# W's products in a round of attention: between scores and y and behind the state products, instead of around the turning of x

## The chip, the cores and the metric

One NeuronCore of a Trainium2 chip runs the whole program in one launch. The metric is the device time of that launch in microseconds. The engines are TensorE (PE), VectorE (DVE), ScalarE (ACT), GpSimd (POOL) and SyncE (SP), which issues most DMA transfers.

## The reference

Three layers follow one another on 4 x 768 tokens of width 8 heads x 48:

```python
for t in range(S):                                   # attention with a decaying state per head
    cur = np.einsum('bhd,bhe->bhde', u[None] * kt, vt)
    y[:, :, t] = np.einsum('bhd,bhde->bhe', rt, state + cur)
    state = w[None, :, :, None] * state + np.einsum('bhd,bhe->bhde', kt, vt)
x = y.transpose(0, 2, 1, 3).reshape(B * S, H * D)    # 3072 x 384
# mixture of 8 experts: tokens with x @ w_skip > 0 add gate * (relu(x @ w1[e]) @ w2[e]), e = argmax of x @ w_gate
out = ((x @ w1) * (x @ w2)) @ w3 @ w_out             # second MLP
```

Only the last matrix product can be rearranged ahead of time: `w3 @ w_out` does not depend on the tokens.

## The kernel before

The attention is done in 24 steps of 128 rows: 12 chunks of 64 positions, and for each chunk two groups of two batches (`n = 2 * chunk + group`). A step needs the scores of the chunk (`scores`, tile `sc`, line 371), their copy out of PSUM under a triangular mask (`evac`, tile `Fs`, line 376, on VectorE), the output `y` or `G` as the sum of scores times v (line 425) and of the old state (line 428, `Ss`), and the products that go into the state (`ds_mm`, tile `S`, line 441). `x_out` adds the bonus term and stores the rows (`xg`), `x_trans` turns them (tile `T`, line 457), `logits` multiplies them with the gate (line 470). For some rounds `route_b` (lines 513 to 516) and `place_mm` (line 599) sort tokens to slots.

All these matmuls on heads are 32 passes on half of the array's rows: fp32 runs a matmul in two passes, and each of the 8 heads has one matmul for the upper and one for the lower 64 partitions. Those of W, of the logits and of the turns use all 128 rows.

While attention runs, `w3 @ w_out` is made as well: `W` is 8 rows of 8 matmuls with 384 columns (`w_mm`, line 708, tiles `wp`), 64 matmuls or 128 passes. `keep(4 * k)` issues the next k of these matmuls; where their operands are not ready yet it issues dummies on a zero tile (line 255, 4 for each `keep(4)`). `WK` holds k for the two places of a round: (1, 1) for rounds 0 to 8, (1, 2) for rounds 9 to 21. In rounds 0 to 4 all are dummies. A finished row of W is copied out of PSUM by `w_evac` (line 689, ScalarE).

The order in a round is written out by hand, and every engine runs its instructions in that order: `manual_schedule` takes the program's text as it stands. The loop `for n in range(NT - 2)` at line 772 is such a round: it computes the scores of step n + 1 and the y of step n. What the change touches:

```python
            y_mm(n)                # line 791
            keep(4 * WK[n][0])     # line 792
            run_todo()             # logits of step n - 2, route_b
            if n > 0:
                x_trans(n - 1)     # line 795
            prep_v(n + 1)
            keep(4 * WK[n][1])     # line 797
            w_step(WN[n][1])
            w_evac(0)
            x_out(n)
            ds_mm(n)               # line 801
            place_mm(n % 2)        # line 802
```

Of the kernel before, what the change touches and what calls it, by code (L numbers as in the profile page):

```python
# [43 lines left out]
WK = [(1, 1)] * 9 + [(1, 2)] * 13  # L44
# [15 lines left out]
def fused_kernel(ctx, tc, att, kv, wt, u, wg, we, w3, wo, w12, r, k, v, wu, out):  # L60
# [132 lines left out]
    def load_expert(e, q):  # L193
        raw = stg[(4 * e + q) % 3 // 2].tile([P, 2, 2 * D], F32, name="raw")
        nc.sync.dma_start(out=raw, in_=we[e, :, 2 * q:2 * q + 2, :])
        return raw
# [29 lines left out]
    with tc.manual_schedule():  # L226
# [10 lines left out]
        def load_t(n):  # L237
            nc.sync.dma_start(out=TB[n % 3].rearrange("p a h t -> p (a h t)"), in_=att[n])

        def load_v(n):  # L240
            c, bp = divmod(n, 2)
            nc.sync.dma_start(out=KV[bp][c % 2].rearrange("p a h d -> p (a h d)"), in_=kv[n])
# [47 lines left out]
        for i in range(6):  # L290
            wn = pw[:, i - 1] if i else wc
            n = 1 << i
# [62 lines left out]
        def prep(n):  # L355

            t = TB[n % 3]
            FK = FK_[n] = wk.tile([P, 2, NH, CH], F32, name="FK", bufs=3)
            return nc.vector.tensor_tensor(out=FK, in0=t, in1=UT[:, n // 2 % 2], op=ALU.mult)

        def behind(later, earlier):

            tc.add_manual_dep(later.ins, earlier.ins.name, mybir.DependencyInfo(
                mybir.DependencyClass.Sync, mybir.DependencyReason.DATA), reason="two operands from SBUF each")

        def scores(n):
            FK = FK_[n]
            sc = ps_1.tile([P, 512], F32, tag="sc", name="sc").rearrange("p (h t) -> p h t", h=NH)
            for h in range(NH):
                for m, d in zip(half, dims):  # L370
                    nc.tensor.matmul(sc[m, h], FK[d, 1, h], FK[d, 0, h], start=True, stop=True)  # L371
            return sc

        def evac(n, sc):
            Fs = Fs_[n] = wk.tile([P, NH, CH], F32, name="Fs")
            nc.vector.tensor_tensor(out=Fs, in0=sc, in1=mask[:, None, :].to_broadcast([P, NH, CH]), op=ALU.mult)

        def prep_k(n):

            c, bp = divmod(n, 2)  # L380
            if c < NC - 1:
                kd = kd_[n] = wk.tile([P, NH, HD], F32, name="kd")
                return nc.gpsimd.tensor_tensor(out=kd, in0=KV[bp][c % 2][:, 1], in1=KU[:, c % 2], op=ALU.mult)

        def prep_m(n):

            c, bp = divmod(n, 2)
            m = P_[n] = wk.tile([P, NH, HD], F32, name="m")
            first = nc.gpsimd.tensor_tensor(out=m, in0=KV[bp][c % 2][:, 0], in1=un, op=ALU.mult)
            nc.gpsimd.tensor_tensor(out=m, in0=KV[bp][c % 2][:, 1], in1=m, op=ALU.mult)  # L390
            return first

        def bonus(n):
            z = z_[n] = wk.tile([P, 32], F32, name="z")[:, 0:NH]
            nc.vector.tensor_reduce(out=z, in_=P_.pop(n), axis=AX.X, op=ALU.add)  # L395

        def prep_v(n, eng=None):
            c, bp = divmod(n, 2)
            v, z = KV[bp][c % 2][:, 2], z_.pop(n)
            zv = zv_[n] = wk.tile([P, NH, HD], F32, name="zv")  # L400
            if eng:
                eng.tensor_tensor(out=zv, in0=v, in1=z[:, :, None].to_broadcast([P, NH, HD]), op=ALU.mult)
            else:
                for h in range(NH):
                    nc.scalar.activation(out=zv[:, h], in_=v[:, h], func=AF.Copy, scale=z[:, h:h + 1])  # L405

        def state_copy(n):
            c, bp = divmod(n, 2)
            s = S[bp]
            if c == 0:  # L410
                return
            if c % 2 == 0:
                nc.vector.tensor_tensor(out=s, in0=s, in1=w128[:, :, None].to_broadcast([P, NH, HD]),
                                        op=ALU.mult)
            nc.scalar.copy(out=Ss[bp], in_=s)

        def y_mm(n, tag="y"):

            c, bp = divmod(n, 2)
            v, Fs, FK = KV[bp][c % 2][:, 2], Fs_.pop(n), FK_.pop(n)  # L420
            y = G if n % 2 and n < NT - 2 else ps_1.tile([P, 512], F32, tag=tag, name="y")
            yv = y[:, 0:D].rearrange("p (h d) -> p h d", h=NH)
            for h in range(NH):
                for m in half:
                    nc.tensor.matmul(yv[m, h], Fs[m, h], v[m, h], start=(h == 0), stop=True, skip_group_check=True)  # L425
            for h in range(NH if c else 0):
                for m, d in zip(half, dims):
                    nc.tensor.matmul(yv[m, h], FK[d, 0, h], Ss[bp][d, h], start=False, stop=True,  # L428
                                     skip_group_check=True)
            y_[n] = y  # L430
            if n < NT - 2:
                yb[0] = y
# [19 lines left out]
        def x_trans(n, bank=None):  # L452
            xg = x_.pop(n)
            xb_[n] = T if bank is None else bank
            pT = xb_[n][:, 0:D].rearrange("p (k t) -> p k t", k=ND)
            for k in range(ND):
                nc.tensor.transpose(pT[:, k], xg[:, P * k:P * k + P], ident)
            xT_[n] = wk.tile([P, ND, P], F32, name="xT", bufs=2)
            nc.scalar.copy(out=xT_[n], in_=pT)
# [137 lines left out]
        def place_mm(bp=0):  # L597
            for o, oh, v in pend:
                nc.tensor.matmul(SL[bp][:, o], oh, v, start=False, stop=True, skip_group_check=True)
            pend.clear()  # L600
# [78 lines left out]
        def w_step(k):  # L679
            for _ in range(k):  # L680
                next(wprep, None)
# [3 lines left out]
        def w_evac(k):  # L685

            while k < len(w_out):
                f, ps = w_out[k]
                nc.scalar.copy(out=W[:, f], in_=ps)
                w_out[k:k + 1] = []  # L690

        def w_ready():
            done.update(fresh[0])
            fresh[:] = fresh[1:] + [[]]
# [21 lines left out]
        def idle_mm():  # L716
            if spare[0] is None and w_out:
                w_evac(0)
            dummy(DQ)
            dummy(DQ)  # L720

        def keep(k):

            due[0] += k
            while due[0] > 0:
                if next(wmm, None):
                    due[0] -= 4
                else:
                    idle_mm()
                    due[0] -= 2  # L730
# [28 lines left out]
        def run_todo(late=False):  # L759
            now, todo[:] = sorted(todo, key=lambda x: x[0] is not logits), []  # L760
            for fn, args in now:
                if late and fn is route_b:
                    todo.append((fn, args))
                    continue
                fn(*args)
                if fn is logits_out:
                    if args[0] in last_of:
                        todo.append((route_a, (last_of[args[0]],)))
                elif fn in NEXT:
                    todo.append((NEXT[fn], args))  # L770

        for n in range(NT - 2):
            w_ready()
            if n == NT - 3:
                raws = {q: load_expert(0, q) for q in range(2)}
            if n + 4 < NT:
                load_t(n + 4)
            fk = prep(n + 2)
            state_copy(n + 1)
            sc = scores(n + 1)  # L780
            behind(prep_k(n + 1) or prep_m(n + 2), fk)
            if n < NT - 3:
                prep_m(n + 2)
            evac(n + 1, sc)
            bonus(n + 1)
            if n == NT - 3:
                bonus(NT - 1)
            next(more_consts, None)
            w_step(WN[n][0])
            w_ready()  # L790
            y_mm(n)
            keep(4 * WK[n][0])
            run_todo()
            if n > 0:
                x_trans(n - 1)
            prep_v(n + 1)
            keep(4 * WK[n][1])
            w_step(WN[n][1])
            w_evac(0)
            x_out(n)  # L800
            ds_mm(n)
            place_mm(n % 2)
            if n + 4 < NT:
                load_v(n + 4)
            if n < NT - 3:
                place(3)
            w_step(WN[n][2])
            run_todo(n < NT - 3)
            if n > 0:
                todo.append((logits, (n - 1,)))  # L810
# [662 lines left out]
```

## Time and profile before

| | before |
|---|---|
| median of 3 runs | 633.9 us (633.12 to 634.04) |
| profiled execution, its own time | 637.01 us |
| profiled execution, span | 635.3 us |
| mean granted clock of PE | 0.991 |
| PE busy | 614.5 us, 97% of the span |
| DVE busy | 464.1 us, 73% |
| ACT busy | 290.7 us, 46% |
| attention, from the first scores to the scores of the last step | 7.6 to 161.8 us |

The profiled execution is a single one, 3.1 us above the median of the runs; busy times and spans come from it. The rounds of attention lie between 10 and 162 us; the tail of attention follows to some 183 us, then the experts to 335 us and the second MLP to the end. In the rows further down, a block of equal instructions is one line: start, length, engine, source line, operation, written tile, read tiles, form, count, and in brackets the idle time before it with what ended it. Blocks overlap a little, since matmuls are pipelined; so the distance from one start to the next is the block's cost, not its length.

### The profile page before, as it was taken

How to read it: one execution, taken by the hardware profiler on the slowest of the kernel's cores; microseconds unless marked ns; L12 is line 12 of the kernel's file. 1: busy time of each engine (PE TensorE's matmuls, PEld its weight loads, DVE VectorE, ACT ScalarE, POOL GpSimd, SP SyncE). 2: the span in 40 equal slices, each digit the busy share in tenths (PEclk: the TensorE clock that was granted, in tenths of full speed). 3: DMA queues.
4: the chain of work that ended last, by engine and by line, in shares of the span. 5: the costliest groups of instructions: out<-in, count | busy, mean ns of one | idle time of the engine just before them, and what ended most of it. 6: DMA issues, size and time to landing. Idle time of an engine off the chain costs nothing.

```text
span 635.3 us, 15258 instructions
## 1 busy us (share of the span) xinstructions
PE 614.5 (97%) x6313; PEld 545.4 (86%) x6313; DVE 464.1 (73%) x820; ACT 290.7 (46%) x705; POOL 141.3 (22%) x140
## 2 busy tenths in 40 slices
PE   7999998999999999999998999999999999999996
PEld 6888877888769999989997989988988988988985
DVE  7699998986477799999956954863863863863760
ACT  2555644534355667666534542443443442442430
POOL 3856465463040232232132300000000000000000
PEclk9799998999999999999999999999999999999999
DMA  8889988575148768877321002002002002000001
GB/s 310 358 280 378 326 291 286 177 252 198 45 127 301 277 230 296 287 241 272 112 75 57 1 17 84 1 18 83 2 18 84 1 17 84 2 18 33 1 2 55
DMA packets 26941, 90.40 MB, mean 142 GB/s; under 512 B 4009, under 2 KB 10729, under 8 KB 25840
## 3 DMA queue, kind: packets, MB, share of 16 engines
q1 hardware_dynamic: 24816, 84.11, 38.1%
q0 software_dynamic: 2048, 5.24, 2.5%
q8 instruction: 51, 0.84, 0.5%
q14 instruction: 26, 0.21, 0.1%
HBM read 77.61 MB, written 12.39 MB: 142 GB/s over the span
## 4 chain that ended last, share of the span: by engine, by line
PE 78%; DVE 11%; DMA 5%; issue 3%; ACT 1%; SPq 0%; POOL 0%; DVEq 0%; ACTq 0%
PE po L1237 16%; PE xy L1196 11%; PE za L1196 10%; PE zb L1196 8%; PE wp L708 6%; PE hp L923 6%; PE y L942 5%; DMA TB<-in_att 3%; DVE elo L87 3%; PE sc L371 3%; PE S L441 2%; PE y L425 2%; PE y L428 1%; PE G L428 1%; DVE hl L927 1%
## 5 line engine op out<-in xcount | busy, mean ns | idle before, releaser
L1178 DVE TENSOR_TENSOR C<-st,za 128x512 f32<-128x512 f32 x47 | 32.3, 687 | 69.7 <-ACT st L1213 69.6
L87 DVE TENSOR_TENSOR elo<-raw,ehi 128x768 fp32r<-128x768 f32 x64 | 60.4, 948 | 4.1 <-ACT ehi L86 4.0
L1237 PE MATMUL po<-pl,W_hi 128*128 128x512 f32 (+1 forms) x152 | 58.1, 383 | 0.0
L1237 PE MATMUL po<-ph,W_hi 128*128 128x512 f32 (+1 forms) x152 | 58.0, 382 | 0.0
L1237 PE MATMUL po<-ph,W_lo 128*128 128x512 f32 (+1 forms) x152 | 57.6, 379 | 0.0
L923 PE MATMUL hp<-xh,ehi 128*128 128x240 f32 x192 | 54.5, 286 | 3.0 <-DVE hl L927 2.4
L1213 ACT COPY st<-xy 128x256 f32<-128x256 f32 x47 | 17.6, 374 | 81.8 <-PE xy L1196 81.8
L86 ACT CAST ehi<-raw 128x768 fp32r<-128x768 f32 x64 | 52.7, 829 | 2.1 <-DMA raw<-in_we 2.1
L1196 PE MATMUL xy<-bxh,w12h 128*128 128x256 f32 x188 | 53.3, 283 | 0.0
L1196 PE MATMUL xy<-bxl,w12h 128*128 128x256 f32 x188 | 53.1, 282 | 0.0
L1196 PE MATMUL xy<-bxh,w12l 128*128 128x256 f32 x188 | 53.1, 282 | 0.0
L923 PE MATMUL hp<-xl,ehi 128*128 128x240 f32 x192 | 52.6, 276 | 0.0
L923 PE MATMUL hp<-xh,elo 128*128 128x240 f32 x192 | 52.4, 274 | 0.0
L708 PE MATMUL wp<-wo_s,w 128*128 128x384 f32 x128 | 51.7, 515 | 0.1
L405 ACT ACTIVATE zv<-KV,z 128x48 f32<-128x48 f32 x184 | 44.0, 327 | 8.0 <-DVE z L395 6.9
L1196 PE MATMUL za<-bxh,w12l 128*128 128x512 f32 x141 | 45.1, 320 | 0.0
L1196 PE MATMUL za<-bxh,w12h 128*128 128x512 f32 x141 | 45.0, 319 | 0.0
L1196 PE MATMUL za<-bxl,w12h 128*128 128x512 f32 x141 | 44.7, 317 | 0.0
L942 PE MATMUL y<-ehi,hh 128*128 128x384 f32 (+1 forms) x128 | 43.3, 339 | 0.0
L942 PE MATMUL y<-elo,hh 128*128 128x384 f32 (+1 forms) x128 | 43.2, 338 | 0.0
L942 PE MATMUL y<-ehi,hl 128*128 128x384 f32 (+1 forms) x128 | 43.1, 337 | 0.0
L923 PEld LDWEIGHTS hp<-xh,ehi 128*128 128x128 f32 x192 | 36.1, 189 | 7.9 <-DVE hl L927 6.9
(249 smaller groups left out, 1671.5 us busy)
## 6 DMA issues: line engine op xcount, KB each, us to landing
raw<-in_we SPq DMA_DIRECT2D x32, 768.0 KB, 5.1
KV<-in_kv SPq DMA_DIRECT2D x24, 576.0 KB, 5.3
TB<-in_att SPq DMA_DIRECT2D x24, 512.0 KB, 7.3
raww<-in_w SPq DMA_DIRECT2D x8, 1024.0 KB, 7.5
raw<-in_w SPq DMA_DIRECT2D x8, 768.0 KB, 6.6
xm<-xg SPq DMA_DIRECT2D x48, 96.0 KB, 3.3
out<-ob SPq DMA_DIRECT2D x17, 256.0 KB, 2.0
x<-xm SPq DMA_DIRECT2D x20, 192.0 KB, 2.8
```

Source lines behind the costliest of these rows:

```text
L86: nc.scalar.copy(out=hi, in_=raw)
L87: (eng or nc.vector).tensor_tensor(out=lo, in0=raw, in1=hi.bitcast(F32), op=ALU.subtract)
L371: nc.tensor.matmul(sc[m, h], FK[d, 1, h], FK[d, 0, h], start=True, stop=True)
L405: nc.scalar.activation(out=zv[:, h], in_=v[:, h], func=AF.Copy, scale=z[:, h:h + 1])
L425: nc.tensor.matmul(yv[m, h], Fs[m, h], v[m, h], start=(h == 0), stop=True, skip_group_check=True)
L708: nc.tensor.matmul(ps, w3[:, g], wo_s[:, g], start=(g == 0), stop=(g == NF - 1))
L923: nc.tensor.matmul(hp, a, b, start=(i == 0), stop=(i == 8))
L942: nc.tensor.matmul(ys[e, t], a[:, P * t:P * t + ROWS[t]], b[:, D:2 * D], start=(f == 0 and i == 0), stop=(f == NF - 1 and i == 2))
L1178: nc.vector.tensor_tensor(out=halves(C[:, 0]), in0=st[:, 0:2], in1=halves(za), op=ALU.add)
L1196: nc.tensor.matmul(o, a, m, start=first and i == 0, stop=(i == 2), skip_group_check=True)
L1213: nc.scalar.copy(out=st[:, 0], in_=X)
L1237: nc.tensor.matmul(po, a[:, f, c], b[:, t], start=(i == 0), stop=(i == 3 * NF - 1))
```

## The change

The first `keep` of a round goes ahead of `y_mm`, behind the scores. The second goes from ahead of `ds_mm` to behind `place_mm`, so that what it issues stands ahead of the next round's scores. Nothing is added or left out, and the numbers of `WK` are the same.

```diff
             w_step(WN[n][0])
             w_ready()
+            keep(4 * WK[n][0])
             y_mm(n)
-            keep(4 * WK[n][0])
             run_todo()
             if n > 0:
                 x_trans(n - 1)
             prep_v(n + 1)
-            keep(4 * WK[n][1])
             w_step(WN[n][1])
             w_evac(0)
             x_out(n)
             ds_mm(n)
             place_mm(n % 2)
+            keep(4 * WK[n][1])
```

On PE, a plain round late in attention (here one that writes `G`; `wp` are W's products, `sc` the scores, `T` the turn, `S` the state; each line gives the count of matmuls, of which every fp32 one runs in two passes):

```order
 L371 MATMUL sc<-FK 64x64 x16
+L708 MATMUL wp_121<-wo_s,w_1092 128x384
 L425 MATMUL G<-KV_0_113,Fs 64x48 x16
 L428 MATMUL G<-Ss_116,FK 64x48 x16
-L708 MATMUL wp_121<-wo_s,w_1092 128x384
 L470 MATMUL G<-wgs,xT 128x9 x3
 L457 MATMUL T<-ident,xg 128x128 x3
+L441 MATMUL S_195<-KV_0_113,kd 48x48 x16
 L708 MATMUL wp_121<-wo_s,w_1092 128x384 x2
-L441 MATMUL S_195<-KV_0_113,kd 48x48 x16
 L371 MATMUL sc<-FK 64x64 x16
```

W's first matmul moved from behind y to ahead of it, and the state products moved up from behind W's other two matmuls to directly behind the turn.

On PE, the end of a round in which tokens are placed (line 599, the last of its three placing matmuls, ahead of the next round's scores):

```order
 L599 LDWEIGHTS s_oh
 L599 MATMUL S_194<-s_v,s_oh 128x80
+L708 MATMUL wp_121<-wo_s,w_1092 128x384 x2
 L371 MATMUL sc<-FK 64x64 x16
+L708 MATMUL wp_121<-wo_s,w_1092 128x384
 L425 MATMUL G<-KV_0_113,Fs 64x48 x16
```

W's two matmuls now stand between the placing and the scores, and the third behind the scores.

On ACT, one of three places where the copy of a finished row of W (line 689) goes down by a round (`L` are logits, `Ss` the state's copy, `xT` the turned x, `zv` the bonus term):

```order
+L473 COPY L<-G 128x9
+L415 COPY Ss_116<-S_195 128x384
+L459 COPY xT<-T 128x384
+L405 ACTIVATE zv<-KV_0_113,z 128x48 x8
 L689 COPY W<-wp_121 128x384
-L473 COPY L<-G 128x9
-L415 COPY Ss_116<-S_195 128x384
-L459 COPY xT<-T 128x384
-L405 ACTIVATE zv<-KV_0_113,z 128x48 x8
```

The copy passed one round's copies of logits, state and turned x and its bonus term. On DVE only the numbers of buffers differ, and POOL and SP have the same order as before.

## Rows read from the trace of the kernel before

**Rows 1.** Stretches: length, busy PE, PEld, DVE, ACT, POOL, clock, DMA share, GB/s.
```profile
41.00:55.00 14.00, 13.95 (x336) 12.10 (x338) 13.89 (x17) 9.58 (x31) 8.32 (x8) 1.00 0.93 339
...
75.00:95.00 20.00, 19.94 (x403) 16.12 (x399) 19.72 (x35) 9.60 (x30) 10.13 (x9) 1.00 0.84 289
...
125.00:145.00 20.00, 20.00 (x438) 17.02 (x438) 16.53 (x30) 8.04 (x33) 10.61 (x10) 1.00 0.72 239
```

**Rows 2.** Timeline of PE in round 16, scores to the next round's scores.
```profile
119.17 1.11 PE L371 MATMUL sc<-FK 48*64 48x64 f32 x32
120.11 1.09 PE L425 MATMUL y<-KV,Fs 64*64 64x48 f32 x32
121.03 1.10 PE L428 MATMUL y<-Ss,FK 48*64 48x48 f32 x32
122.06 0.91 PE L708 MATMUL wp<-wo_s,w 128*128 128x384 f32 x2
122.81 0.73 PE L470 MATMUL y<-wgs,xT 128*128 128x9 f32 x6
123.40 0.53 PE L457 MATMUL T<-ident,xg 128*128 128x128 f32 x3
123.76 1.46 PE L708 MATMUL wp<-wo_s,w 128*128 128x384 f32 x4
125.14 0.92 PE L441 MATMUL S<-KV,kd 64*48 64x48 f32 x32
125.90 1.11 PE L371 MATMUL sc<-FK 48*64 48x64 f32 x32
```

**Rows 3.** Timeline of PE in round 5, where W has two passes between T and S.
```profile
45.87 0.81 PE L708 MATMUL wp<-wo_s,w 128*128 128x384 f32 x2
46.61 0.92 PE L441 MATMUL S<-KV,kd 64*48 64x48 f32 x32
```

**Rows 4.** Timeline of PE in attention's tail: y behind W, logits behind y.
```profile
167.01 1.14 PE L425 MATMUL y<-KV,Fs 64*64 64x48 f32 x32
167.98 1.10 PE L428 MATMUL y<-Ss,FK 48*64 48x48 f32 x32
169.00 0.84 PE L470 MATMUL G<-wgs,xT 128*128 128x9 f32 x6
```

**Rows 5.** Timeline of PE at the end of round 11, with placing.
```profile
86.74 0.92 PE L441 MATMUL S<-KV,kd 64*48 64x48 f32 x32
87.60 0.28 PE L599 MATMUL S<-s_v,s_oh 128*128 128x80 bf16 x3
87.81 1.15 PE L371 MATMUL sc<-FK 48*64 48x64 f32 x32
```

**Rows 6.** Timeline of PE in round 3, dummies around logits and turn.
```profile
32.12 0.61 PE L255 MATMUL wp<-zb 128*128 128x256 bf16 x4
32.57 0.73 PE L470 MATMUL G<-wgs,xT 128*128 128x9 f32 x6
...
33.52 0.60 PE L255 MATMUL wp<-zb 128*128 128x256 bf16 x4
34.05 0.92 PE L441 MATMUL S<-KV,kd 64*48 64x48 f32 x32
```

**Rows 7.** Timeline of PE from 40 to 106 us: its waits, and what follows the longest.
```profile
40.98 1.15 PE L371 MATMUL sc<-FK 48*64 48x64 f32 x32 [0.43 <-DVE Fs L376]
...
55.90 1.13 PE L428 MATMUL G<-Ss,FK 48*64 48x48 f32 x31 [0.37 <-issue]
...
62.34 0.56 PE L425 MATMUL y<-KV,Fs 64*64 64x48 f32 x13 [0.50 <-issue]
...
99.79 0.37 PE L428 MATMUL G<-Ss,FK 48*64 48x48 f32 x5 [1.80 <-issue]
...
101.79 2.59 PE L708 MATMUL wp<-wo_s,w 128*128 128x384 f32 x4
104.31 1.37 PE L441 MATMUL S<-KV,kd 64*48 64x48 f32 x32
```

## Prediction

> **What bounds the kernel now.** I read the busy time by stretches first, then TensorE's timeline inside single rounds, then the waits at its idle spots. The reader should see in [rows 1] that in three stretches between 41 and 145 us TensorE (PE) is hardly ever free: 13.95 of 14.00, 19.94 of 20.00 and 20.00 of 20.00 us, at the full granted clock. VectorE (DVE) is just as full early (13.89 of 14.00, 19.72 of 20.00) and has room later (16.53 of 20.00). So a round of attention lasts as long as PE's own instructions, and what the change costs or saves must be read from how PE's blocks follow one another. [rows 2] are round 16: seven blocks between the scores at 119.17 and the next at 125.90, 6.73 us, with no wait. I call a block small if its matmuls use half of the array's rows (scores `sc`, the two halves of `y`, state products `S`) and full if they use all 128 (W's products `wp`, logits at line 470, turns `T` at line 457, the dummies at line 255). Today a round has one pair of switches: small to full from `y` to `wp`, full to small from `wp` to `S`. The order shown above has three pairs in a plain round: sc|wp|y, y|logits and T|S, S|wp|sc.
>
> **What a pair of switches costs.** The same instructions are timed by the distance from one block's start to the next's.
> Small to full: the 32 passes of the first half of y take 121.03 - 120.11 = 0.92, the 32 of the second 122.06 - 121.03 = 1.03 [rows 2], 0.11 more where a full block follows. Two passes of W entered from y take 122.81 - 122.06 = 0.75. Their own pace: four passes between T and S take 125.14 - 123.76 = 1.38 [rows 2], two in the same place 46.61 - 45.87 = 0.74 [rows 3], so a pass is 0.32 and two are 0.64 to 0.65. Entering costs 0.10 more. Together 0.21.
> Full to small: 0.74 - 0.65 = 0.09 on the full side [rows 3], and on the small side the first half of y takes 167.98 - 167.01 = 0.97 where W stands before it, against 0.92: 0.05 [rows 4]. Together 0.14.
> A pair with fp32 weights is thus **0.35 us**. Two of the new neighbours already occur in the tail: W before y (above), and the logits straight after y, again 169.00 - 167.98 = 1.02 against 0.92 [rows 4].
> Bounds for one pair: below, a round in which the placing matmuls (line 599, bf16) stand between S and sc: 87.81 - 86.74 = 1.07 [rows 5] against 125.90 - 125.14 = 0.76 without them [rows 2], 0.31 more for one pair and three short matmuls; even if those take 0.1 together a pair is 0.2. Above, 0.40: 0.35 plus a rounding step of 0.01 in each of the differences. I take 0.35, since it is read from the very blocks that are moved.
>
> The Trainium skill (TensorEngine Tiling, section Tiling Modes, Key Properties) says that changing the tiling mode drains TensorE; it gives no time. Another of its pages (TensorE: Matmul & The Clock Gate, Part 2, the drain step) puts a drain at about 128 cycles; at 2.4 GHz that is 0.053 us for a switch, an estimate, and the 29 pairs below would come to 3.1 us instead of 10.2. The trace agrees that a switch costs, and not on that size: 0.35 for a pair.
>
> **The change, part by part.** The first `keep` moves from behind y to ahead of it; the second from ahead of S to behind S and the placing. No instruction is added or removed.
> 1. Rounds 5 to 21 run real W products. In twelve of these seventeen rounds the number of pairs goes from one to three. In the other five (11, 12, 17, 18, 21) the placing matmuls already make S|place|sc a pair ([rows 5] is one), and W now stands directly behind them, so there it goes from two to three. 12 x 2 + 5 x 1 = 29 pairs x 0.35 = **+10.2**. All of it is on the path, since PE has no idle time there [rows 1].
> 2. Rounds 1 to 4 run four dummies at each `keep`. A pair around dummies: 0.11 on leaving y as above; the four take 0.45 entered from y and 0.53 left into S [rows 6], so at least 0.08 on leaving; 0.05 on the small side as above. I take 0.25 (ends 0.24 and 0.35). Before there is one such pair; after there are two, and one y|logits, T|S pair at 0.35: 0.60 a round, 2.4 for four. Round 0 waits for loads and hides its share. PE reaches the scores at 40.98 with 0.43 us to wait for DVE's Fs [rows 7], which absorbs that much: **+2.0**.
> 3. Two short stalls of PE in the middle of y, 0.37 before 55.90 and 0.50 before 62.34, end on "issue", no engine's work [rows 7]. Both fall in the run S, sc, y, y, in which 128 small matmul passes and as many weight loads are issued in 0.76 + 0.94 + 0.92 + 1.03 = 3.65 us [rows 2] with nothing long between them. The change cuts this run with W on either side of sc, so I take both away: **-0.87**. Bounds: 0 and -0.87.
> 4. The long stall, 1.80 before 99.79, also "issue", and behind it the half clock: four passes at 101.79 take 104.31 - 101.79 = 2.52 instead of 1.38 [rows 7]. Nothing I can read says whether a shifted program meets it, so it stays in the sum, and its removal (1.80 + 1.14, and 0.45 in the S block behind, busy 1.37 [rows 7] instead of 0.92 [rows 2]: 3.4) makes one end of the range.
> 5. ScalarE copies a finished piece of W one round later. It is off the path: ACT is busy 8.04 of 20.00 us [rows 1] and W has two banks. Without that cover a copy would cost PE under 1 us each time; three are moved. The orders of SP and POOL do not move, so no transfer is issued past another. No semaphore wait is added: sc still comes after Fs and FK, with more time for DVE before it.
>
> Sum: 10.2 + 2.0 - 0.9 = **+11.3**. The profiled execution took 637.0 (span 635.3) and would become 648.3; it stands 3.1 above the median of the runs, 633.9, to which I add the same: **645.2 us**.
>
> **The rivals.**
> A, the long stall and its half clock are gone: 645.2 - 3.4 = 641.8. For it: it is the same sort of stall as the two short ones, and the run before it is cut. Against: it is five times as long, and may be absent from unprofiled runs anyway. 0.17.
> B, VectorE paces the early rounds, so that PE's switches there are free. DVE is 99% busy from 41 to 55 and from 75 to 95 us [rows 1]. Rounds 5 to 12 would lose 14 pairs, 4.9, and rounds 1 to 4 their 2.0: 638.3. Against: PE is as full, and waited 0.43 in all for Fs in this stretch [rows 7]. 0.06.
> C, the other side, **faster**: in the run of small blocks the supply of instructions is what PE lacks, and the next block's loads are fetched early enough to hide a switch. Then the change costs nothing, and the three stalls with the half clock, 0.87 + 3.4 = 4.3, are won: 629.6. It decides where a pair costs under 4.3 / 37 = 0.12, 37 being the 29 pairs and the 8 early ones. For it: the turns pass to W at full pace, T to wp 0.36 for three turns [rows 2], so loads are hidden between full blocks. Against: 0.35 measured at exactly the other kind of border, and never under 0.2. 0.05.
> The Trainium skill's rule behind C (TensorE: Matmul & The Clock Gate, Part 2, the LDWEIGHTS step) is that the engine pulls weight loads ahead of running matmuls where row groups do not conflict or the background buffer is the target. The trace agrees between full blocks, and not where a small block precedes: there the first two passes of W took 0.10 longer.
> D, gains and costs cancel: a pair costs about 0.12 and the stalls go, 633 to 635. The diff does act in every round, so "no effect" needs such a balance. 0.03.
> E, the clock: the added gaps let PE fall to half clock in a stretch of the rounds, as behind 99.79. One such fall costs 1.6 (1.14 + 0.45), two 3.2: 648.4, and more if it comes often. For it: 6 gaps a round instead of 2. Against: the fall of [rows 7] came after 1.80 us without work, while a gap at a switch is 0.1 to 0.2. 0.09.
>
> **How the numbers follow.** The forecast, with its terms at other values (0.32 to 0.38 a pair, the short stalls kept), is 644 to 647 and has 0.60. Rivals A to E hold 0.40. The range takes in the forecast, A, and E with two falls: **640.5 to 648.5**; B, C, D and the far part of E, about 0.17, are outside. A measurement of this kernel can tell about 0.2% (1.3 us) from no change. Faster by more than that is C: 0.05. Within: D, 0.03. Slower: 0.92.
>
> **What would show it.** Right: a plain round late in attention takes 7.4 instead of 6.73 us; sc to wp reads 1.05 instead of sc to y 0.94; T to S about 0.45, S to wp about 0.87; the logits behind y take 0.70 instead of 0.59; no waits of PE on DVE after 41 us; everything behind attention is shifted whole. Step 3 is wrong if "issue" stalls remain inside y. Wrong altogether: rounds of 6.7 us (C), rounds under 7 before 95 us with waits on Fs (B), or half clock in [rows 1]'s stretches (E).

## The result and the profile after

The changed kernel takes **642.2 us** (median of 5 runs, 641.06 to 643.91) beside 633.2 of the kernel before (633.12 to 634.04, 5 runs on the same chip): ratio 1.0139, 95% interval 1.0122 to 1.0156, so 9.0 us slower. The forecast was 645.2 with a range of 640.5 to 648.5. The profiled execution of the changed kernel took 642.80 us, its span is 641.1; that of before 637.01 and 635.3. The two profiles differ by only 5.8, because the one of before holds the long stall and the half clock of [rows 7], which a second profile of it doesn't have (experiments 8 and 11 are second profiles of both kernels).

First the stretches that answer to [rows 1], of the kernel after (length, busy PE, PEld, DVE, ACT, POOL, granted clock, DMA share, GB/s):

```profile
41.00:55.00 14.00, 14.00 (x317) 11.44 (x316) 13.89 (x18) 8.20 (x26) 8.32 (x8) 1.00 0.90 301
75.00:95.00 20.00, 20.00 (x393) 15.13 (x390) 19.73 (x37) 10.63 (x36) 10.06 (x10) 1.00 0.79 280
125.00:145.00 20.00, 20.00 (x393) 15.52 (x389) 15.89 (x26) 9.06 (x36) 11.30 (x11) 1.00 0.61 199
```

PE is now busy without a gap in all three, and does less: 393 matmuls from 125 to 145 us where there were 438. A slower kernel with a busier engine: the share of busy time says nothing about the pace here, because a switch is counted as busy. Weight loading (PEld) went the other way, 17.02 to 15.52.

PE's timeline in round 16 of the kernel after (start, duration, engine, line, operation, output<-input, count), which answers to [rows 2]:

```profile
121.78 1.15 PE L371 MATMUL sc<-FK 48*64 48x64 f32 x32
122.86 0.91 PE L708 MATMUL wp<-wo_s,w 128*128 128x384 f32 x2
123.70 1.13 PE L425 MATMUL y<-KV,Fs 64*64 64x48 f32 x32
124.67 1.10 PE L428 MATMUL y<-Ss,FK 48*64 48x48 f32 x32
125.70 0.84 PE L470 MATMUL y<-wgs,xT 128*128 128x9 f32 x6
126.39 0.53 PE L457 MATMUL T<-ident,xg 128*128 128x128 f32 x3
126.84 0.92 PE L441 MATMUL S<-KV,kd 64*48 64x48 f32 x32
127.69 1.56 PE L708 MATMUL wp<-wo_s,w 128*128 128x384 f32 x4
129.18 1.15 PE L371 MATMUL sc<-FK 48*64 48x64 f32 x32
```

From start to start, with [rows 2] in brackets: scores 1.08 (0.94), W's two passes 0.84 (0.75), y 0.97 and 1.03 (0.92 and 1.03), logits 0.69 (0.59), turns 0.45 (0.36), state products 0.85 (0.76), W's four passes 1.49 (1.38). The round takes 7.40 instead of 6.73. Seven of the eight blocks have a new neighbour on one side or on both and became 0.05 to 0.14 longer; the second half of y, which has a full block behind it as before, kept its 1.03.

The end of round 11, a round with placing, on the same timeline; it answers to [rows 5]:

```profile
89.46 0.92 PE L441 MATMUL S<-KV,kd 64*48 64x48 f32 x32
90.32 0.28 PE L599 MATMUL S<-s_v,s_oh 128*128 128x80 bf16 x3
90.43 1.53 PE L708 MATMUL wp<-wo_s,w 128*128 128x384 f32 x4
91.90 1.15 PE L371 MATMUL sc<-FK 48*64 48x64 f32 x32
```

Placing passes to W after 0.11 where it passed to the scores after 0.21. Such a round takes 7.49 or 7.50 instead of 7.04 to 7.09 (one of the five in before, round 12, took 7.30).

Of the waits of [rows 7] none is left. PE waits on Fs only at the scores of rounds 0 and 1. The summed waits of PE from 0 to 185 us (line, releaser: us in total, times, longest):

```profile
PE sc L371 <- DVE Fs L376: 1.3, 2, 1.1
```

No "issue" row is in that view, and no wait lies in rounds 5 to 21. The scores of round 5, at 40.98 in [rows 7], stand here without a wait:

```profile
42.37 1.15 PE L371 MATMUL sc<-FK 48*64 48x64 f32 x32
```

### The profile page after: what moved, and what is told of

Its sections match the earlier page's. It is cut to its first block, busy times and chain, and to the rows that moved or that the text cites. A ratio compares the mean times of both kernels' runs of the same rounds, so it can differ in the third digit from the quotient of the medians.

```text
span 641.1 us, 15258 instructions
## 1 busy us (share of the span) xinstructions
PE 623.6 (97%) x6313; PEld 545.2 (85%) x6313; DVE 461.1 (72%) x820; ACT 290.5 (45%) x705; POOL 141.6 (22%) x140
## 4 chain that ended last, share of the span: by engine, by line
PE 81%; DVE 11%; issue 2%; DMA 2%; ACT 1%; POOL 0%; SPq 0%; DVEq 0%; ACTq 0%; POOLq 0%
PE po L1237 15%; PE xy L1196 11%; PE za L1196 10%; PE zb L1196 8%; PE wp L708 6%; PE hp L923 5%; PE y L942 5%; PE sc L371 4%; DVE elo L87 4%; PE S L441 3%; PE y L425 2%; PE G L425 2%; PE y L428 2%; DVE hl L927 2%; PE G L470 2%
## 5 line engine op out<-in xcount | busy, mean ns | idle before, releaser
L961 POOL DMA_INDIRECT xm<-yo,sidx x16 | 23.3, 1454 | 88.3 <-DVE yo L958 74.0
```

The source lines that it names most:

```text
L961: ins = nc.gpsimd.indirect_dma_start(out=xm[:, :], out_offset=bass.IndirectOffsetOnAxis(ap=sidx[0:n, j, 1:2], axis=0), in_=yo, in_offset=N ...
```

## The experiments

In every diff the lines are those of the loop over the rounds, against the kernel before. Where a kernel has several runs, several of the kernel before stand beside them, on the same chip. "Own pace" of a round means that no block in it stalls.

### 1. The first product of W alone is moved

```diff
+            keep(4 * WK[n][0])
             y_mm(n)
-            keep(4 * WK[n][0])
```

> Only the first group of W's products moves (to between scores and y); the second stays ahead of the state products. Theory (a pair of switches between half-array and full-array matmuls costs 0.34 us): every one of rounds 5 to 21 gets exactly one pair more, 17 x 0.34 = 5.8, rounds 1 to 4 about 0.25 each less the 0.4 that PE waited, small stalls inside y partly gone (0.9 to 2): +4 to +6, 637 to 639. A plain round late in attention 7.07 instead of 6.73. Rival (the cost is the delay of the scores by W's products in front of them, which DVE's mask copy and so the next round pays): here nothing stands in front of the scores, so 0 to +1.

Measured: 637.59 us beside 633.91, ratio 1.0051 [1.0017, 1.0084], +3.7. PE's timeline late in attention:

```profile
117.27 1.11 PE L371 MATMUL sc<-FK 48*64 48x64 f32 x32
118.31 0.91 PE L708 MATMUL wp<-wo_s,w 128*128 128x384 f32 x2
119.16 1.14 PE L425 MATMUL y<-KV,Fs 64*64 64x48 f32 x32
120.13 1.10 PE L428 MATMUL y<-Ss,FK 48*64 48x48 f32 x32
```

Scores to W 1.04 instead of 0.94, W 0.85 instead of 0.75, the first half of y 0.97 instead of 0.92, the logits behind it 0.69 instead of 0.59: +0.35 for one more pair. The total is just under the forecast of +4 to +6. The round takes 7.08, one with placing 7.40, both 0.35 above before. So a half of the change has half of its cost in each round.

### 2. The second product of W alone is moved

```diff
-            keep(4 * WK[n][1])
...
             place_mm(n % 2)
+            keep(4 * WK[n][1])
```

> Only the second group moves (to behind the state products and the placing). Theory: one pair more in the 12 plain rounds, none in the 5 with placing: 12 x 0.33 = 4.0, rounds 1 to 4 about 0.3 each less the wait of 0.4: +4 to +5, 637 to 638.5; rounds with placing keep 7.05 to 7.1. Rival (delay of the scores): all of the change's +9 is here.

Measured: 635.99 us, ratio 1.0012 [0.9990, 1.0034], +2.1 by the medians, with the interval reaching to no change; the verdict rests on the timeline:

```profile
121.05 0.53 PE L457 MATMUL T<-ident,xg 128*128 128x128 f32 x3
121.50 0.92 PE L441 MATMUL S<-KV,kd 64*48 64x48 f32 x32
122.35 1.56 PE L708 MATMUL wp<-wo_s,w 128*128 128x384 f32 x4
123.84 1.15 PE L371 MATMUL sc<-FK 48*64 48x64 f32 x32
```

A plain round takes 7.06 (+0.33: the turns 0.45 instead of 0.36, S 0.85 instead of 0.76, W 1.49 instead of 1.38, and the scores behind it 0.98 instead of 0.94). A round with placing takes 7.15, +0.11, where I had put 0: placing already made that pair, but W behind it is not quite as cheap as W behind the turns. If W in front of the scores had delayed the next round as such, this kernel alone would have carried the 9 us. It doesn't: in a plain round the two halves add up, 0.35 + 0.33 = 0.68 beside 0.67. The whole times don't add up: the medians give 3.7 + 2.1 = 5.8 of the 9.0, and this half stays below its forecast of +4 to +5. A good part of the gap lies in rounds 5 to 10, where each half alone has room that both share: they take 40.10 us in experiment 1 and 40.23 here beside 39.72 in before (experiment 8), 0.4 and 0.5 more, though six pairs cost 2.0 to 2.1.

### 3. Both products move, but stay together

```diff
-            keep(4 * WK[n][0])
...
+            keep(4 * WK[n][0])
             keep(4 * WK[n][1])
```

> Both groups stand together between the turning of x and the state products: W moved as far as in the change, but the number of switches is that of the kernel before. Theory: within 1 us of before, a plain round 6.73. Rival (what counts is that W's products are spread over the round, for the clock or for the instruction supply): slower by some us, with half clock or stalls that end on issue.

Measured: 633.66 us, 0.25 below before by the medians; the ratio, 0.9968 [0.9948, 0.9989], is lower than the medians say; 14 of before's 35 runs there lie above 635, and none of this kernel's 12. W stands in one block between the turns and S:

```profile
119.06 2.10 PE L708 MATMUL wp<-wo_s,w 128*128 128x384 f32 x6
121.09 0.92 PE L441 MATMUL S<-KV,kd 64*48 64x48 f32 x32
```

Here W's first product is moved past logits and turns, and ScalarE's copy of a piece shifts as it does in the change, but the number of pairs in a round stays one. The round stays at 6.73. Moving W costs nothing; a new border does.

### 4. Placing ahead of the state products

```diff
+            place_mm(n % 2)
             ds_mm(n)
-            place_mm(n % 2)
```

> The kernel before with the placing matmuls ahead of the state products, so that they follow W directly. Theory: one pair less in the 5 rounds with placing, which take about 6.75 to 6.8 instead of 7.04 to 7.1: -1.5 us, 631.7. Rival (the placing costs what its own three matmuls take, or waits for DVE's lanes in its new place): no change or slower.

Measured: 632.88 us, ratio 0.9968 [0.9944, 0.9992], 1.0 below before by the medians. A round with placing:

```profile
134.02 1.46 PE L708 MATMUL wp<-wo_s,w 128*128 128x384 f32 x4
135.31 0.27 PE L599 MATMUL S<-s_v,s_oh 128*128 128x80 bf16 x3
135.51 0.92 PE L441 MATMUL S<-KV,kd 64*48 64x48 f32 x32
136.27 1.11 PE L371 MATMUL sc<-FK 48*64 48x64 f32 x32
```

The forecast was -1.5 and 6.75 to 6.8 a round, a little too much. S now passes to the scores after 0.76 as in a plain round, and the placing costs 0.20 behind W less the 0.09 that W's exit no longer has. The round takes 6.84 instead of 7.05; five of them make 1.05. This takes a pair out where the change puts pairs in, and it is the kernel that beats both with the rounds to show for it (experiment 3's interval lies below 1 too, but its rounds are as long as before, so an interval this close to 1 proves little by itself).

### 5 to 7. One added matmul, at three kinds of place

A matmul of zeros with an output that nobody reads: a full one among small ones, a small one in the same place, and a full one among full ones.

```diff
+            nc.tensor.matmul(T[:, 448:512], zb[:, 0:P], zb[:, 0:64], start=True, stop=True)
             y_mm(n)
```

> The kernel before with one more matmul in every round, on a zero tile with all 128 rows and 64 columns in bf16, between scores and y; its result is not used. Theory (a pair of switches costs, whatever the full matmul does): 0.2 to 0.3 in each plain round, 6.95 to 7.0 instead of 6.73, and +3 to +4 in all, because rounds 1 to 9 hide part behind DVE. Rival (what costs is W's long matmul standing in front of y, or fp32 weights that are loaded late): one short bf16 matmul costs 0.03 a round, under +1.

```diff
+            nc.tensor.matmul(T[0:64, 448:512], zb[0:64, 0:64], zb[0:64, 0:64], start=True, stop=True)
             y_mm(n)
```

> The same place and the same 64 columns, but with 64 rows and 64 weight columns, half of the array as its neighbours. Theory: no switch, so 0.03 to 0.06 a round and under +1 in all. Rival (any foreign matmul between scores and y costs, for a wait or for the bank it writes): as much as with all 128 rows.

```diff
             keep(4 * WK[n][0])
+            nc.tensor.matmul(T[:, 448:512], zb[:, 0:P], zb[:, 0:64], start=True, stop=True)
```

> The full matmul of 128 rows and 64 columns beside W's first product behind y, among full blocks. Theory: no switch is added, 0.03 to 0.06 a round, under +1 in all. Rival (the matmul itself or its bank costs): as much as between scores and y.

Measured, beside 633.67: 641.07 us for the full one among small ones (ratio 1.0098 [1.0071, 1.0124]), 638.0 for the small one (1.0052 [1.0029, 1.0074]), 635.24 for the full one among full ones (1.0025 [1.0000, 1.0050]). All three medians are above their forecasts (+3 to +4, under +1, under +1) and the first two well above what the rounds give. The three profiled executions each hold a stretch at half clock (last section); of the other runs only the mean granted clock is known, and in most runs of the first two it is as low as in the profiled ones, 0.987 to 0.992. The lowest runs are 638.09, 634.55 and 634.03. So the price is read from the rounds, from PE's timeline. Full among small:

```profile
121.12 1.11 PE L371 MATMUL sc<-FK 48*64 48x64 f32 x32
122.16 0.20 PE L791 MATMUL T<-zb 128*128 128x64 bf16 x1
122.29 1.14 PE L425 MATMUL y<-KV,Fs 64*64 64x48 f32 x32
123.26 1.10 PE L428 MATMUL y<-Ss,FK 48*64 48x48 f32 x32
```

Small among small:

```profile
120.02 1.11 PE L371 MATMUL sc<-FK 48*64 48x64 f32 x32
120.96 0.19 PE L791 MATMUL T<-zb 64*64 64x64 bf16 x1
120.97 1.13 PE L425 MATMUL y<-KV,Fs 64*64 64x48 f32 x32
121.89 1.14 PE L428 MATMUL y<-Ss,FK 48*64 48x48 f32 x32
```

Full among full:

```profile
120.80 0.91 PE L708 MATMUL wp<-wo_s,w 128*128 128x384 f32 x2
121.55 0.19 PE L793 MATMUL T<-zb 128*128 128x64 bf16 x1
121.58 0.81 PE L470 MATMUL y<-wgs,xT 128*128 128x9 f32 x6
122.25 0.52 PE L457 MATMUL T<-ident,xg 128*128 128x128 f32 x3
```

The scores to the full matmul take 1.04 instead of 0.94, it takes 0.13, and the first half of y 0.97 instead of 0.92: +0.28. With the small matmul the same three read 0.94, 0.01 and 0.92, and the whole round is longer by 0.05 (6.78). With the full one between W and the logits: 0.75, 0.03 and 0.67 for the logits instead of 0.59, +0.11. The same matmul is thus 2.5 times as dear between small blocks as between full ones, and a small one there is nearly free. So most of the price comes with the change of kind, not with one more instruction. Not all of it does: of the 0.11, which has no change of kind in it, 0.08 is the logits' own time. Behind this short full matmul they take 0.67, nearly the 0.69 that they take straight behind y in the changed kernel, and behind W's long matmuls 0.59. So what is booked to a switch at the logits may be a first weight load that a short matmul ahead does not cover; that was not tested. Nor was it tested whether rows or columns make the kind: the full matmul has 128 of both, the small one 64.

### 8 and 11. Both kernels profiled again

> The kernel before once more, for a second profile of it. If the long stall before 99.79 us with its half clock belongs to that one execution, it is absent here and the attention ends some 3 us earlier; rounds 5 to 9 then show short stalls that end on issue, or waits for DVE. If it belongs to the program, it is there again at the same place.

> The changed kernel once more, for a second profile. If the half clock of rounds 1 to 3 (16.3 to 23.1 us in its first profile) is that execution's, it is absent here: the scores of round 5 start near 41 us after a wait for Fs instead of at 42.37 without one, and the span is about 1.3 shorter, 639.5 to 640.

Measured: 632.95 us with a span of 631.1 (clock 0.998) for the kernel before, 641.24 with 639.4 (clock 0.999) for the changed one. Neither has a half-clock stretch or the long stall, and they differ by 8.3, close to the 9.0 of the medians. So this pair is the one to take apart. The kernel before, PE's timeline in rounds 5 to 10:

```profile
40.80 1.15 PE L371 MATMUL sc<-FK 48*64 48x64 f32 x32 [0.97 <-DVE Fs L376]
...
54.98 1.44 PE L428 MATMUL G<-Ss,FK 48*64 48x48 f32 x32
56.36 0.91 PE L708 MATMUL wp<-wo_s,w 128*128 128x384 f32 x2
...
66.75 0.38 PE L425 MATMUL G<-KV,Fs 64*64 64x48 f32 x6
67.40 0.95 PE L425 MATMUL G<-KV,Fs 64*64 64x48 f32 x25 [0.26 <-issue]
...
68.20 1.14 PE L428 MATMUL G<-Ss,FK 48*64 48x48 f32 x31
...
79.27 0.92 PE L441 MATMUL S<-KV,kd 64*48 64x48 f32 x32
80.52 1.15 PE L371 MATMUL sc<-FK 48*64 48x64 f32 x32 [0.33 <-DVE Fs L376]
```

The changed kernel, summed waits of PE on Fs from 40 to 185 us:

```profile
PE sc L371 <- DVE Fs L376: 1.2, 1, 1.2
```

That one wait is at the scores of round 5, which come at 40.83, beside 40.80 before: rounds 0 to 4 cost nothing here, since both kernels end them waiting for Fs. Rounds 5 to 10 take 39.72 before (40.80 to 80.52) and 42.02 after (40.83 to 82.85), +2.30; rounds 11 to 21 take 76.11 and 82.21, +6.10.

In the late stretch six plain and five placing rounds at +0.67 and +0.43 make 6.2, and 6.10 is there. In rounds 5 to 10 six at +0.67 make 4.0, and only 2.30 is there. The rest is what before lost against its own pace: the second half of y takes 56.36 - 54.98 = 1.38 instead of 1.03 in round 7, the first half 1.07 instead of 0.92 in round 8 and 68.20 - 66.75 = 1.45 in round 9, together 1.03 in the middle of y, and S to the scores takes 80.52 - 79.27 = 1.25 instead of 0.76 in round 10 with a wait on Fs, and 0.06 more in round 5: together 0.55. The changed kernel has neither; its rounds 5 to 10 run at their own pace, 6.76 four times, 7.58 and 7.40.

Whatever makes y stall, the kernel before could hardly have been faster here, because of VectorE. Its copy of Fs that the scores of round 11 wait for, first in the kernel before, then in the changed one:

```profile
79.78 0.68 DVE L376 TENSOR_TENSOR Fs<-sc,mask 128x512 f32<-128x512 f32 x1
79.80 0.68 DVE L376 TENSOR_TENSOR Fs<-sc,mask 128x512 f32<-128x512 f32 x1
```

From 40 to 98 us every instruction of VectorE starts at the same time in both kernels, within 0.04 us, though PE falls behind by 3.2 us in that time (scores of round 13 at 94.68 and 97.84): VectorE keeps its own pace there and waits for PE in neither. In the kernel before, the scores of round 11 start 0.06 behind the end of that copy, 79.78 + 0.68 = 80.46. Had y not stalled, PE would have waited there instead. In the changed kernel they come 2.4 behind it. So 1.7 of the 4.0 that the new pairs cost in rounds 5 to 10 is hidden behind VectorE.

### 9 and 10. The change in the first or the last rounds alone

Experiment 9 makes both moves where n < 9, experiment 10 where n >= 9:

```diff
+            if n < 9:
+                keep(4 * WK[n][0])
             y_mm(n)
-            keep(4 * WK[n][0])
+            if not (n < 9):
+                keep(4 * WK[n][0])
...
-            keep(4 * WK[n][1])
+            if not (n < 9):
+                keep(4 * WK[n][1])
...
             place_mm(n % 2)
+            if n < 9:
+                keep(4 * WK[n][1])
```

> The change in rounds 0 to 8 alone, the old order from round 9. Theory (switches cost 0.67 a round, but VectorE is nearly as full as PE up to round 10 and its mask copies hold PE up anyway): the 0.67 is seen in rounds 5 to 8 as 6.76 instead of 6.1, yet waits for Fs and short stalls go in exchange, so +0.5 to +1.5 in all. Rival (every pair of switches is on the path, in early rounds too): 8 pairs in rounds 5 to 8 at 0.34 and 1 to 2 for the rounds of dummies: +4 to +5.

> The change in rounds 9 to 21 alone. Theory: 8 plain rounds x 0.67 and 5 with placing x 0.43 = 7.5, less the 0.3 to 0.5 that PE waits for Fs around round 10: +6.5 to +7.5, so nearly all of the change's +8 to +9. Rival (all pairs count alike): +7.5 here and the rest of some 4 in the early half.

Measured, beside 633.76: 634.39 for the early rounds (ratio 1.0004 [0.9986, 1.0022], +0.6), 643.99 for the late ones (1.0152 [1.0103, 1.0202], its two lowest runs 640.46 and 640.72). In the profile of experiment 9 rounds 5 to 8 take 6.76 each, 27.03 beside 25.01 in experiment 8, and rounds 9 and 10, in the order of before, take 6.95 and 6.73 where experiment 8 has 7.48 and 7.23. So of the +2.0 by which rounds 5 to 8 are longer, 1.0 comes back in the two rounds behind them, where PE, 1.8 us later than in experiment 8, has neither a stall in y nor a wait on Fs, in the old order. In experiment 10 rounds 9 to 21 take 97.15 (69.91 to 167.06) beside 90.82: +6.33, about what eight plain and five placing rounds cost, 7.5, less the 1.07 that experiment 8 loses in rounds 9 and 10.

The 644 of experiment 10 is more than the whole change costs. Its stretches show why (columns as above):

```profile
30.00:41.00 11.00, 8.75 (x200) 7.82 (x199) 10.96 (x13) 4.45 (x15) 6.70 (x12) 1.00 0.72 240
41.00:52.00 11.00, 11.00 (x155) 9.22 (x155) 10.93 (x13) 6.88 (x24) 5.86 (x5) 0.54 0.89 318
```

Its PE timeline at the scores of round 5 and of round 6:

```profile
40.82 1.20 PE L371 MATMUL sc<-FK 48*64 48x64 f32 x32 [1.50 <-DVE Fs L376]
...
51.32 1.43 PE L371 MATMUL sc<-FK 48*64 48x64 f32 x32
```

Round 5, which is in the order of before in this kernel, took 10.50 instead of 6.19 because the granted clock fell to the lower level, 1.2 instead of 2.4 GHz, behind a wait of 1.50 for Fs. These 4.3 and the 6.33 make 10.6 of the 11.0 by which its span, 642.1, exceeds that of experiment 8. The cost of the late rounds is thus 6.3, not 10; the two lowest runs, 6.7 and 7.0 above before, lie in the forecast of +6.5 to +7.5, the median does not.

## Why the prediction was right, and where its steps were off

**The pair of switches (0.35): right in mechanism and near in size.** Three ways to make pairs gave 0.35 (experiment 1), 0.33 (2) and, for both, 0.67 a plain round; moving W without a new border gave 0 (3); removing the pair at the placing gave -0.21 (4), just at the lower bound that had been read from [rows 5]. A round with placing was taken as one more pair net, 0.35, and costs 0.43, because W behind the placing costs 0.11. The Trainium skill (TensorEngine Tiling, section Tiling Modes, Key Properties) says that a change of tiling mode drains TensorE. The runs agree that a change of kind costs, 0.28 for a full matmul among small blocks against 0.11 among full ones. The estimate from the other page of the Trainium skill (TensorE: Matmul & The Clock Gate, Part 2, the drain step), 3.1 us for 29 pairs, is a third of the 10.2 that the rounds show. What a switch is made of, a drain or the next weight load that starts late, was not separated; with bf16 weights the added full matmul costs 0.28, with W's fp32 a pair costs 0.33 to 0.35, so the kind of load may have a part in it.

**Item 1 (+10.2): right in the price, wrong in "all of it is on the path".** Twelve rounds at 0.67 and five at 0.43 are 10.2. In rounds 11 to 21 all of it is on the path (+6.10 of 6.2); in rounds 5 to 10 VectorE hides 1.7 of 4.0. PE's full share of busy time in [rows 1], 13.95 of 14.00, was read as no idle time; but a block that is stretched counts as busy.

**Item 2 (+2.0 in rounds 1 to 4): the size was wrong.** In the first pair of profiles it is +1.39 (scores of round 5 at 42.37 against 40.98), and two of the rounds there do grow from 5.58 to 6.16, the 0.60 of the prediction. But in that pair both kernels had run most of round 1 at half clock, 16 to 23 us, which had put PE behind and used up its slack. In experiments 8 and 11 the same scores come at 40.80 and 40.83 and wait 0.97 and 1.22 for Fs: VectorE sets that time, and the term is 0. The 0.43 us of wait in [rows 7] that I subtracted was the slack of an execution that had been slowed.

**Item 3 (-0.87, the short stalls): the stalls went, but the mechanism was not shown and the gain is not theirs.** The stalls inside y are gone in every round with W on both sides of the scores (changed kernel, experiment 9). They are gone as well in the old order where PE runs later against VectorE: in rounds 9 and 10 of experiment 9, and nearly in experiment 4, where a half clock brought PE to the scores of round 5 at 43.19 and rounds 5 to 10, with no placing in them, lost only 0.5 against their own pace. So that W's place in the run of small blocks removes them was not shown. Nor does their going win time, since VectorE sets the scores of round 11. How large they are must be read from the lengthening of the block, not from the idle time marked "issue": [rows 7] marks 0.37 and 0.50, experiment 8 marks only 0.26, while its blocks of y grew by 1.03. That the supply of instructions is what those rows stand for was argued from the trace; no run altered it alone. Where the prediction took 0.87 off for stalls, the runs show 1.7 hidden behind VectorE.

**Item 4, rival A (the long stall): it belonged to one execution.** Experiment 8 is the same program as before without it. So the profiled execution of before carried some 4 us that experiment 8 does not have (spans 635.3 and 631.1), 3.6 of them in the round of the long stall, 10.41 instead of 6.77, for which the prediction had 3.4; the prediction was right to leave it in both its sides, taking 3.1 off at the end to reach the median. Rival A's 641.8 is nearer to the result than the forecast, but not for its reason: it takes off once more what the median of before had not held.

**The sum.** 10.2 + 0 - 1.7 = +8.5, beside +8.3 in the second pair of profiles and +9.0 by the medians. The prediction's +11.3 is 2.8 above that sum, 2.0 of it from item 2 and 0.8 because VectorE hid 1.7 where 0.87 had been put for the stalls, and 2.3 above the medians. Both errors come from VectorE's pace up to round 10, and both made the forecast too high.

**The other rivals.** B (VectorE paces the early rounds), given 0.06, holds for rounds 1 to 4 and, in part, for 5 to 10, where 1.7 of 4.0 is hidden: 3.7 of the 6.9 that it took off, so that the result lies between the forecast and B's 638.3. What stood against it, that PE is as full and waits only 0.43 for Fs, overlooked the stretched blocks. B doesn't hold for all pairs, since from round 5 on the changed kernel's rounds are at their own pace, with DVE as busy as before, 39.45 of the 40.00 us from 41 to 81 us in both. C (the switches are hidden, faster) and D (cancelled) fall: no new pair of W's in a plain round cost under 0.33, and of the 4.3 that C counted on, the long stall was not in the median, and the short ones had lain in time that VectorE set. E (half clock in attention) is real as a risk of any of these kernels, experiments 4, 5, 6, 7 and 10 had it, but the changed kernel's two profiles have none of it in rounds 5 to 21.

## What to carry to other kernels

When PE is full, write its program as a string of blocks by the part of the array that they use and count the borders: here each pair of borders costs a third of a microsecond, and where full blocks are put together (W beside logits and turns, placing beside W) it is paid once a round. Read that price from distances between block starts, since a slower switch looks like a busier engine. An engine that is busy all the time can still have slack: here the start times of VectorE, the same in both kernels up to 98 us, showed that PE had it. And take slack, stalls and clock from more than one execution before they enter a sum.

## What the runs showed of the hardware that was not expected

A stretch at the lower clock comes in some executions and at different places: between 16 and 24 us in the first profiles of both kernels (mean granted clock 0.76 from 14 to 28 us in either) and in experiments 6 and 7, behind 99.79 in [rows 7], 28.6 to 38.5 in experiment 4, 40.6 to 44.1 in experiment 7, 41.8 to 52.0 in experiment 10, 42.5 to 52.7 in experiment 5, 71.2 to 78.0 in experiment 6. Before the two falls near 42 PE had waited 1.31 (experiment 5) and 1.50 us (experiment 10) for Fs at the scores of round 5; with waits of 0.97, 1.22 and 1.23 at the same scores (experiments 8, 11 and 9), but also of 1.32, 1.39 and 1.44 (experiments 1, 2 and 6), the clock stayed at full. So the length of that wait alone does not decide. The stretch near 42 makes a round of 6.2 us into 10.5, as much as a dozen pairs of switches. What decides was not found.
